# Attention and a feed-forward network in one kernel: the loop over attention units, with a unit's scores and another unit's sums in one run of TensorE

## The chip, the cores and the metric

The kernel runs on one core of one Trainium2 chip. The metric is the device time of one execution in microseconds (us); less is better. Engines are named as the profile names them: PE is TensorE's matmuls and PEld its weight loads, DVE is VectorE, ACT is ScalarE, POOL is GpSimd, and SP is the engine that issues the DMAs.

## The reference

For each of 8 batches and 8 heads there are 576 queries, keys and values of 64 numbers. Scores are masked by blocks of 64 (a query sees the keys of its own block and of earlier ones), go through a softmax, and weigh the values. The heads' results side by side are the rows `x` of a feed-forward network with SiLU.

```python
scores = scale * np.matmul(q, k.transpose(0, 1, 3, 2))          # q, k, v: 8 x 8 x 576 x 64
scores = np.where(block_i >= block_j, scores, -1e9)             # blocks of 64
attn = np.exp(scores - scores.max(-1)); attn /= attn.sum(-1) + 1e-09
x = np.matmul(attn, v).transpose(0, 2, 1, 3).reshape(4608, 512)
h = x @ w_in                                                    # 512 x 2048
out = (h / (1 + np.exp(-h))) @ w_out                            # 2048 x 512
```

## The kernel before

Every fp32 operand of a matmul is split into a high part in TensorE's own 32-bit format and a low part, the rest; a product is then two or three matmuls (high by high, high by low, low by high). ACT makes a high part by a cast (`split_hi`, `v_hi`, `p_hi`, `x_hi`, `g_hi`), and POOL makes the low part by a subtraction (`split_lo`, `v_lo`, `p_lo`, `x_lo`, `g_lo`).

**Attention.** One of 64 units is one head of one batch, for its last 448 queries (the first 128 are done elsewhere, early). A unit's keys stand in five chunks of 128, and only the queries that see a chunk are computed, so its scores are five segments (`SEG`) with 448, 320, 192, 448 and 64 columns, which lie in three PSUM banks (`BANKS`). Its steps are, in the order in which they depend on one another:

- `load`, `split_hi`, `split_lo`: queries and keys, one buffer each for the raw and the split ones;
- `scores`: 10 matmuls on PE into the three banks (each segment with the high and the low part of the queries);
- `max`, `max2`, `sub` on DVE: the maximum over 32 queries at a time, and the difference, into the one tile `T`;
- `exp` on ACT into the tile `p`, one bank at a time; `sums`, and for each second unit `sums2`, on DVE add up `p`;
- `p_hi`, `p_lo`: the two parts `ph` and `pl` of `p`; `load_v`, `v_hi`, `v_lo`: the two parts of the values, in one tile `vc`;
- `pv`: 9 matmuls on PE (`PV`: segment, part of `p`, and how many columns of weights) that sum the values into one PSUM bank `U`;
- `lower` on ACT and `fold` on DVE join the two halves of `U`; `mult` on DVE, for two units at once, divides by the sums (it uses the bank `U` for the spread reciprocals); `x_hi` and `x_lo` write the pair's rows of `x`.

**The feed-forward network** goes over 18 blocks of 256 tokens in 8 steps each. A step is four groups on PE of about equal length: two of `ffn1` (12 matmuls with 256 columns each, from `x` into a PSUM tile `h`, of which there are two), and two of `ffn2` (6 matmuls with 512 columns each, into `o`), these two steps behind the first (`LAG`). Between them are `silu` and `g_hi` on ACT and `g_lo` on POOL (one tile `g`, two tiles `g2`), and at a block's end `output` and `store`. `ffn(n)` issues the next `n` groups with what lies between them.

**Order.** Every engine's queue is in the order of the program, which is fixed (`manual_schedule`). The string `ORDER` is written out by hand and holds the whole beginning: the weights, the first 128 queries, units 0 to 16 in part, and 156 groups of the network. From unit 17 (`TABLE`) on a loop issues one unit per iteration `i`: the scores of unit `i`, the sums of unit `i-1`, the end of unit `i-2`, and 6 or 7 groups of the network (`pace`, from the number of groups issued so far). Groups that are left come behind the loop. A block of the network can start when the last unit that holds its tokens is through `x_lo`.

**Tiles.** `p`, `ph` and `pl` are asked for anew in each unit, under a tag with one buffer: the first write of a new tile waits until every reader of the old one is done. Within one tile waits go by what overlaps.

The lines of the profile: L306 the scores, L385 the sums, L618 `ffn1`, L648 `ffn2`, L250 `max` and `sums`, L259 and L321 and L254 `max2` (L254 also `mult`), L336 to L338 `sub`, L347 `exp`, L353 `p_hi`, L361 and L363 `p_lo`, L278 `split_hi`, L282 and L284 `split_lo`, L290 and L293 `v_hi` and `v_lo`, L390 `lower`, L396 `fold`, L401 `mult`, L418 and L422 `x_hi` and `x_lo`, L625, L631 and L636 `silu`, `g_hi` and `g_lo`, L656 and L661 `output` and `store`.

Of the kernel before, what the change touches and what calls it, by code (L numbers as in the profile page):

```python
# [9 lines left out]
F32 = mybir.dt.float32  # L10
F32R = mybir.dt.float32r
# [3 lines left out]
ALU = mybir.AluOpType  # L15
# [3 lines left out]
B, H, S, D = 8, 8, 576, 64  # L19
DM, DFF = 512, 2048  # L20
P = 128
NQ = S - 2 * D
# [4 lines left out]
NFF = DFF // P  # L27
NSTEP = NFF // 2
TB = 256
CT = DM // P  # L30
NX = 16
EVEN = 4
AHEAD = 152
TABLE = 17
# [3 lines left out]
SEG = [(0, 0, 0, 448), (2, 448, 128, 320), (3, 768, 256, 192), (1, 960, 0, 448), (4, 1408, 384, 64)]  # L38
COLS = 1472

QK = [0, 1, 3, 2, 4]
PV = [(0, 0, 128), (1, 0, 128), (2, 0, 128), (2, 1, 64), (1, 1, 64), (0, 1, 64), (4, 0, 128), (3, 1, 64), (3, 0, 128)]
BANKS = [(0, 448), (448, 960), (960, 1472)]


# [85 lines left out]
def attn_ffn(ctx: ExitStack, tc: tile.TileContext, qk, v, qk0, v0, qk1, v1, w_in, w_out, out):  # L131
    nc = tc.nc
    pool = lambda name, bufs=1, **kw: ctx.enter_context(tc.tile_pool(name=name, bufs=bufs, **kw))
    cp = pool("const")
    sp = pool("work")
    pS = pool("pS", space=PSUM)

    def bank(i):
        return pS.tile([P, 512], F32, tag=f"S{i}", name=f"S{i}")

    pU = pool("pU", space=PSUM)
    pH = pool("pH", bufs=2, space=PSUM)
# [15 lines left out]

    xbuf = cp.tile([P, NX, 2, TB], F32R, name="x")
    x_free = list(range(NX))  # L160
# [3 lines left out]
    ready = set()  # L164
# [91 lines left out]
    def quad_fold(X, src, op):  # L256

        for a in range(4):
            nc.vector.tensor_reduce(out=X[:, :, a], in_=src[32 * a : 32 * a + 32], axis=AX.X, op=op)  # L259

    class Unit:


# [28 lines left out]
        def v_lo(u):  # L292
            nc.gpsimd.tensor_tensor(out=u.vc[:, :, 64:], in0=u.v3, in1=u.vc[:, :, :64], op=ALU.subtract)  # L293

        def scores(u):
            banks = [bank(0), bank(1), bank(2)]

            def ps(c, w, r=P):
                i = max(i for i in range(3) if BANKS[i][0] <= c)
                return banks[i][:r, c - BANKS[i][0] : c - BANKS[i][0] + w]  # L300

            u.ps = ps
            for j, c, q0, w in (SEG[i] for i in QK):
                m = min(P, S - j * P)
                for i, qq in enumerate((u.qh, u.ql)):
                    nc.tensor.matmul(u.ps(c, w, m), u.kk[:, j * P : j * P + m], qq[:, q0 : q0 + w], start=i == 0, stop=i == 1)  # L306

        def max(u):
            ttr(Mx[:, :, 0], blocks32(u.ps(0, NQ)), ALU.max)
# [25 lines left out]
        def sub(u):  # L335
# [4 lines left out]
                    u.half_sub(0)  # L340
            u.half_sub(1)

        def exp(u, k):
            if k == 0:
                u.p = sp.tile([P, COLS], F32, tag="p", name="p")
            c, e = BANKS[k]
            nc.scalar.activation(u.p[:, c:e], T[:, c:e], AF.Exp, scale=SCALE)  # L347

        def p_hi(u, k):
            if k == 0:  # L350
                u.ph = sp.tile([P, COLS], F32R, tag="ph", name="ph")
            c, e = BANKS[k]
            nc.scalar.copy(u.ph[:, c:e], u.p[:, c:e])  # L353

        def p_lo(u, k):

            if k == 0:
                u.pl = sp.tile([P, COLS], F32R, tag="pl", name="pl")
            c, e = BANKS[k]
            e = min(e, SEG[-1][1])  # L360
            nc.gpsimd.tensor_tensor(out=u.pl[:, c:e], in0=u.p[:, c:e], in1=u.ph[:, c:e], op=ALU.subtract)  # L361
            if k == 2:
                nc.gpsimd.tensor_tensor(out=u.ph[64:, e:], in0=u.p[:64, e:], in1=u.ph[:64, e:], op=ALU.subtract)  # L363
# [13 lines left out]
            u.rr = sp.tile([P, NQB], F32, tag="rr", name="rr")  # L377
            nc.vector.reciprocal(out=u.rr, in_=rs)

        def pv(u):  # L380

            U = u.U = pU.tile([P, 512], F32, tag="U", name="U")[:, :NQ]
            for n, (i, pp, m) in enumerate(PV):
                j, c, q0, w = SEG[i]
                nc.tensor.matmul(U[:m, q0 : q0 + w], u.vc[:, j, :m], (u.ph, u.pl)[pp][:, c : c + w], start=n == 0, stop=n == 8)  # L385

        def lower(u):
            a = u.a
# [51 lines left out]
    class Early:  # L440
# [40 lines left out]
        def tiles(u, blk, n):  # L481

            for c in range(CT):
                if (blk, c) not in x_tiles:
# [3 lines left out]
            t = x_tiles[blk, 0]  # L488
            assert [x_tiles[blk, c] for c in range(CT)] == list(range(t, t + CT))
            return xbuf[:, t : t + CT]  # L490

    class First(Early):
# [145 lines left out]
    def ffn2(blk, d, t):  # L638
        g2 = gs[blk, d]
        if d == 0 and t == 0:  # L640
            outs[blk] = [bank(2), pU.tile([P, DM], F32, tag="U", name="o1")] if blk == 0 else [pO.tile([P, DM], F32, tag="o", name="o") for _ in range(2)]
        o = outs[blk][t]
        tk = slice(t * P, t * P + P)
        n = 0
        for f in range(2):
            assert ("out", d, f) in ready
            for gt, wt in ((0, 0), (0, 1), (1, 0)):
                nc.tensor.matmul(  # L648
                    o, g2[:, gt, f, tk], wo[wt][:, 2 * d + f, :],
                    start=d == 0 and n == 0, stop=d == NSTEP - 1 and n == 5,  # L650
                )
                n += 1

    def output(blk, d, t):
        ot = sp.tile([P, DM], F32, tag="ot", name="ot", bufs=2)
        (nc.vector.tensor_copy if late else nc.scalar.copy)(ot, outs[blk][t])  # L656
        outs[blk][t] = ot

    def store(blk, d, t):
        for i, r, w in rows(blk, t):  # L660
            nc.sync.dma_start(out=out[r : r + w, :], in_=outs[blk][t][i : i + w, :])  # L661
# [16 lines left out]
    steps += [(blk, d) for blk in range(2, B * S // TB) for d in range(NSTEP)]  # L678


    work_list = []
# [12 lines left out]
    late = []  # L694
# [24 lines left out]
    units = [Unit(b, h) for b in range(B) for h in range(H)]  # L719
# [11 lines left out]
    for token in ORDER.split():  # L731
        name, _, method = token.partition(".")
        if name.startswith("warm:"):
            warm(int(name[5:]))
        elif method:
            method, _, k = method.partition(":")
# [3 lines left out]
        else:  # L740
            do(name)
    n = len(units)
    for i in range(TABLE, n + 2):
        u = units[i] if i < n else None
        w = units[i - 1] if i <= n else None
        z = units[i - 2] if i > TABLE else None
        pace = 6 + (count[0] <= AHEAD + 7 * (i - TABLE))
        if u:
            u.scores()
            u.max()  # L750
        if z:
            z.fold()
            if z.h % 2:
                z.mult()
        if u:
            u.max2()
        if i + 1 < n:
            units[i + 1].split_hi()
            units[i + 1].split_lo()
            if i + 2 < n:  # L760
                units[i + 2].load()
        ffn(pace - 3)
        if z and z.h % 2:
            z.x_hi()
            z.x_lo()
        if w:
            w.sums()
            w.pv()
        if u:
            u.v_hi()  # L770
            u.v_lo()
            if i + 1 < n:
                units[i + 1].load_v()
            u.sub()
        if w:
            w.lower()
        if u:
            for part in (u.exp, u.p_hi, u.p_lo):
                for k in range(3):
                    part(k)  # L780
        if w and w.h % 2:
            w.sums2()
        late.append(u)
        ffn(3)
        late.pop()
    ffn(10000)


# [38 lines left out]
```

## Time and profile before

| | |
|---|---|
| time, median of 3 runs | 1043.84 us (1043.38 to 1045.03) |
| time of the profiled execution | 1043.46 us |
| span of its profile | 1041.7 us |
| busy: PE, PEld | 1033.4 us (99%), 939.7 us (90%) |
| busy: DVE, ACT, POOL | 763.5 us, 749.1 us, 750.0 us (72 to 73%) |
| granted clock of PE | 1.00 in every slice |

The time is that of the whole execution, and the span goes from the first to the last instruction of its profile. A timeline's row has the start in us from the start of the span, the time from the start of its first to the end of its last instruction, the engine, the line, the operation with the tiles that it writes and reads, and how many instructions in a row it stands for; in brackets stands how long the engine was idle before, and what ended that. A matmul's row lasts longer than the distance to the next one's start, since matmuls are pipelined: it is the starts that show PE's pace.

### The profile page before, as it was taken

What the parts mean: (1) busy time and instruction counts of PE and PEld (TensorE: products, weight loads), DVE (VectorE), ACT (ScalarE), POOL (GpSimd) and SP (SyncE); (2) the same over time, 40 slices, a digit from 0 to 9 for tenths busy, and PEclk for the clock granted to TensorE, in tenths of its full rate; (3) what the DMA queues carried; (4) which work ended last, traced back from release to release, by engine and by line L of the source; (5) the groups of instructions that cost most, each with busy time, mean ns of one, the idle gap of its engine ahead of it and who ended that gap; (6) DMA issues with size and microseconds to landing.
All of it is one profiled execution on the core that took longest, in us unless ns stands there. A gap on an engine that the chain in (4) does not pass through costs nothing.

```text
span 1041.7 us, 20247 instructions
## 1 busy us (share of the span) xinstructions
PE 1033.4 (99%) x7176; PEld 939.7 (90%) x7176; DVE 763.5 (73%) x2232; ACT 749.1 (72%) x1194; POOL 750.0 (72%) x726
## 2 busy tenths in 40 slices
PE   8999999999999999999999999999999999999998
PEld 8988899999899999999999999998999999989987
DVE  7998489999978988888878888888888888700000
ACT  5876578898797888787878787878787777722222
POOL 5766579898897878787878787878787878622221
PEclk9999999999999999999999999999999999999999
DMA  8876223222322222222322222222222222000000
GB/s 291 260 247 189 63 75 90 52 67 74 92 50 84 54 54 74 55 77 59 85 56 74 59 75 55 64 64 54 74 54 75 54 74 54 27 1 21 1 21 21
DMA packets 35044, 79.95 MB, mean 77 GB/s; under 512 B 4736, under 2 KB 12928, under 8 KB 34944
## 3 DMA queue, kind: packets, MB, share of 16 engines
q1 hardware_dynamic: 34944, 78.66, 26.9%
q8 instruction: 57, 0.93, 0.4%
q14 instruction: 43, 0.35, 0.1%
HBM read 69.21 MB, written 9.44 MB: 75 GB/s over the span
## 4 chain that ended last, share of the span: by engine, by line
PE 87%; DVE 4%; POOL 3%; ACT 2%; DMA 2%; issue 1%; SPq 0%; DVEq 0%; POOLq 0%; ACTq 0%
PE h L618 35%; PE o L648 35%; PE S L306 8%; PE U L385 8%; DVE S L227 1%; DVE wm L233 1%; DVE S L223 1%; DMA wst<-in_moe_w_in_dram 1%; POOL pl L361 1%; POOL g L636 1%; DMA T<-in_moe_w_in_dram 0%; PE S L648 0%; ACT L625 0%; DMA qkraw<-in_qk_dram 0%; POOL qh L282 0%
## 5 line engine op out<-in xcount | busy, mean ns | idle before, releaser
L618 PE MATMUL h<-x,wi 128*128 128x256 f32 x3456 | 441.6, 282 | 0.9 <-ACT g L625 0.6
L618 PEld LDWEIGHTS h<-x,wi 128*128 128x128 f32 x3456 | 430.2, 189 | 12.7 <-ACT g L625 1.0
L648 PE MATMUL o<-wo,g 128*128 128x512 f32 x1680 | 424.3, 397 | 0.0
L648 PEld LDWEIGHTS o<-wo,g 128*128 128x128 f32 x1680 | 305.9, 188 | 62.6 <-issue 0.2
L361 POOL TENSOR_TENSOR pl<-p,ph 128x448 fp32r<-128x448 f32 (+1 forms) x192 | 226.0, 1202 | 93.9 <-ACT ph L353 93.5
L636 POOL TENSOR_TENSOR g<-g,g 128x512 fp32r<-128x512 f32 x144 | 186.4, 1295 | 119.8 <-ACT g L631 115.2
L250 DVE TRANSPOSE_TENSOR_REDUCE Mx<-S 64x4 f32<-64x128 f32 (+4 forms) x384 | 135.7, 405 | 94.0 <-PE S L306 93.9
L625 ACT ACTIVATE g<-h 128x512 f32<-128x512 f32 x144 | 86.1, 598 | 126.0 <-POOL g L636 74.6
L631 ACT CAST g<-g 128x512 fp32r<-128x512 f32 x144 | 89.3, 620 | 60.1 <-PE o L648 58.2
L250 DVE TRANSPOSE_TENSOR_REDUCE Dx<-p 128x14 f32<-128x448 f32 (+3 forms) x320 | 122.6, 446 | 0.1
L347 ACT ACTIVATE p<-T 128x512 f32<-128x512 f32 (+1 forms) x192 | 105.6, 604 | 9.5 <-POOL ph L363 8.5
L353 ACT CAST ph<-p 128x512 fp32r<-128x512 f32 (+1 forms) x192 | 104.4, 596 | 1.3 <-PE U L385 1.1
L282 POOL TENSOR_TENSOR qh<-qkraw,qh 64x576 fp32r<-64x576 f32 x64 | 91.6, 1431 | 15.8 <-ACT qh L278 7.1
L306 PE MATMUL S<-qh 128*128 128x448 f32 (+3 forms) x320 | 90.5, 296 | 0.0
L625 ACT ACT_TABLE_LOAD x66 | 84.7, 1283 | 1.4 <-PE h L618 0.3
L306 PE MATMUL S<-ql,qh 128*128 128x448 f32 (+3 forms) x320 | 84.1, 307 | 0.0
L347 ACT ACT_TABLE_LOAD x62 | 79.5, 1283 | 1.6 <-DVE Dx L250 0.5
L284 POOL TENSOR_TENSOR ql<-qkraw,qh 128x448 fp32r<-128x448 f32 x64 | 74.1, 1157 | 5.1 <-PE S L594 0.2
L385 PE MATMUL U<-ph,vc 128*128 128x448 f32 (+3 forms) x320 | 74.1, 297 | 0.0
L278 ACT CAST qh<-qkraw 128x1024 fp32r<-128x1024 f32 x64 | 66.9, 1045 | 8.8 <-PE S L306 4.1
L338 DVE TENSOR_TENSOR T<-S,MR 128x256 f32<-128x256 f32 (+2 forms) x192 | 73.0, 406 | 0.0
L293 POOL TENSOR_TENSOR vc<-vraw,vc 128x320 fp32r<-128x320 f32 x64 | 56.2, 878 | 13.3 <-ACT vc L290 12.8
(120 smaller groups left out, 1120.4 us busy)
## 6 DMA issues: line engine op xcount, KB each, us to landing
qkraw<-in_qk_dram SPq DMA_DIRECT2D x128, 256.0 KB, 3.9
vraw<-in_v_dram SPq DMA_DIRECT2D x64, 160.0 KB, 2.3
wst<-in_moe_w_out_dram SPq DMA_DIRECT2D x15, 512.0 KB, 4.6
out_dram<-ot SPq DMA_DIRECT2D x24, 256.0 KB, 2.9
wst<-in_moe_w_in_dram SPq DMA_DIRECT2D x10, 512.0 KB, 5.3
v<-in_v_dram SPq DMA_DIRECT2D x12, 256.0 KB, 5.2
qk<-in_qk_dram SPq DMA_DIRECT2D x8, 384.0 KB, 5.3
T<-in_moe_w_in_dram SPq DMA_DIRECT2D x6, 512.0 KB, 4.5
```

The source lines that it names most:

```text
L250: nc.vector.tensor_reduce(out=out, in_=in_, axis=AX.X, op=op, apply_transpose=True)
L282: nc.gpsimd.tensor_tensor(out=u.qh[64:, NQ:], in0=u.raw[64:, NQ:], in1=u.qh[64:, NQ:], op=ALU.subtract)
L306: nc.tensor.matmul(u.ps(c, w, m), u.kk[:, j * P : j * P + m], qq[:, q0 : q0 + w], start=i == 0, stop=i == 1)
L347: nc.scalar.activation(u.p[:, c:e], T[:, c:e], AF.Exp, scale=SCALE)
L353: nc.scalar.copy(u.ph[:, c:e], u.p[:, c:e])
L361: nc.gpsimd.tensor_tensor(out=u.pl[:, c:e], in0=u.p[:, c:e], in1=u.ph[:, c:e], op=ALU.subtract)
L385: nc.tensor.matmul(U[:m, q0 : q0 + w], u.vc[:, j, :m], (u.ph, u.pl)[pp][:, c : c + w], start=n == 0, stop=n == 8)
L618: nc.tensor.matmul(h[:, f, :], wi[wt][:, c, w], x[:, xt, :], start=n == 0, stop=n == 3 * CT - 1)
L625: nc.scalar.activation(g, hs.pop((blk, d)), AF.Silu)
L631: nc.scalar.copy(g2[:, 0], g)
L636: nc.gpsimd.tensor_tensor(out=g2[:, 1], in0=g, in1=g2[:, 0], op=ALU.subtract)
L648: nc.tensor.matmul(o, g2[:, gt, f, tk], wo[wt][:, 2 * d + f, :], start=d == 0 and n == 0, stop=d == NSTEP - 1 and n == 5,)
```

## The change

- `scores` of unit `i` takes the unit two before it along: seven of that unit's nine sums come ahead of the ten scores, and two behind them, in another order (`JOINT`). The loop's sums are thus those of unit `i-2`, not of unit `i-1`, and the run of sums by itself is gone (it stays for the last two units).
- `p`, `ph` and `pl` become three tiles that the loop keeps (`place`), so a write of one bank's columns waits only for the readers of those columns. `p_hi` and `p_lo` go by banks 1, 0, 2.
- In an iteration the queues now hold: `max`, `max2`; then `v_hi`, `v_lo`, `load_v`, `p_hi`, `p_lo` of unit `i-1` (they were those of unit `i`, behind `exp`); `lower`, `fold` of unit `i-2`; one group; `split_hi`, `sub`, `split_lo`, `load`; `mult`; one group; `x_hi`, `x_lo`; all groups but four; `sums`; `exp`; two groups; `sums2`.
- The copies of `output` go to DVE only in the part with all groups but four.
- The very last `ffn2` group is done in two parts of 256 columns: the left one goes on in its bank, the right one's last sums go to a bank of their own. ACT copies the first bank out, DVE adds the right part, and each half has its own store.

```diff
+JOINT = [(0, 0, 128), (2, 0, 128), (2, 1, 64), (1, 1, 64), (1, 0, 128), (4, 0, 128), (3, 1, 64), (0, 1, 64), (3, 0, 128)]
...
-        def scores(u):
+        def scores(u, other=None):
...
+            if other is not None:
+                other.pv(JOINT[:7])
+            for i in QK:
+                j, c, q0, w = SEG[i]
                 m = min(P, S - j * P)
...
+            if other is not None:
+                other.pv(JOINT[7:], 7)
...
+        def place(u, tag, kind):
+
+            if tag not in places:
+                t = sp.tile([P, COLS], kind, tag=tag, name=tag)
+                if not keep:
+                    return t
+                places[tag] = t
+            return places[tag]
...
-            if k == 0:
-                u.p = sp.tile([P, COLS], F32, tag="p", name="p")
+            if not hasattr(u, "p"):
+                u.p = u.place("p", F32)
...
-        def pv(u):
-
-            U = u.U = pU.tile([P, 512], F32, tag="U", name="U")[:, :NQ]
-            for n, (i, pp, m) in enumerate(PV):
+        def pv(u, products=PV, first=0):
+
+            if first == 0:
+                u.U = pU.tile([P, 512], F32, tag="U", name="U")[:, :NQ]
+            for n, (i, part, m) in enumerate(products, first):
                 j, c, q0, w = SEG[i]
-                nc.tensor.matmul(U[:m, q0 : q0 + w], u.vc[:, j, :m], (u.ph, u.pl)[pp][:, c : c + w], start=n == 0, stop=n == 8)
+                nc.tensor.matmul(u.U[:m, q0 : q0 + w], u.vc[:, j, :m], (u.ph, u.pl)[part][:, c : c + w], start=n == 0, stop=n == 8)
...
         tk = slice(t * P, t * P + P)
...
+        split = t and (blk, d) == (NBLK - 1, NSTEP - 1)
+        if split:
+            outs[blk][t] += [(bank(0)[:, :HD], slice(HD, DM))]
+        for i, (o, c) in enumerate(outs[blk][t]):
+            if split and i == 0:
+                o, c = o[:, :HD], slice(0, HD)
...
+        (o, c), *right = outs[blk][t]
+        (nc.vector.tensor_copy if late else nc.scalar.copy)(ot, o)
+        outs[blk][t] = [(ot, c)]
+        for o, c in right:
+            nc.vector.tensor_tensor(out=ot[:, c], in0=o, in1=ot[:, c], op=ALU.add)
+            outs[blk][t] = [(ot, slice(0, HD)), (ot, c)]
...
+    keep.append(True)
     for i in range(TABLE, n + 2):
         u = units[i] if i < n else None
-        w = units[i - 1] if i <= n else None
+        w = units[i - 1] if TABLE < i <= n else None
         z = units[i - 2] if i > TABLE else None
         pace = 6 + (count[0] <= AHEAD + 7 * (i - TABLE))
         if u:
-            u.scores()
+            u.scores(z)
             u.max()
+            u.max2()
+        else:
+            z.pv()
+        if w:
+            w.v_hi()
+            w.v_lo()
+            if u:
+                u.load_v()
+            for part in (w.p_hi, w.p_lo):
+                for k in (1, 0, 2):
+                    part(k)
         if z:
+            z.lower()
             z.fold()
-            if z.h % 2:
-                z.mult()
-        if u:
-            u.max2()
+        ffn(1)
         if i + 1 < n:
             units[i + 1].split_hi()
+        if u:
+            u.sub()
+        if i + 1 < n:
             units[i + 1].split_lo()
             if i + 2 < n:
                 units[i + 2].load()
-        ffn(pace - 3)
+        if z and z.h % 2:
+            z.mult()
+        ffn(1)
+        late.append(u)
         if z and z.h % 2:
             z.x_hi()
             z.x_lo()
-        if w:
-            w.sums()
-            w.pv()
+        ffn(pace - 4)
+        if i <= n:
+            units[i - 1].sums()
         if u:
-            u.v_hi()
-            u.v_lo()
-            if i + 1 < n:
-                units[i + 1].load_v()
-            u.sub()
-        if w:
-            w.lower()
-        if u:
-            for part in (u.exp, u.p_hi, u.p_lo):
-                for k in range(3):
-                    part(k)
-        if w and w.h % 2:
-            w.sums2()
-        late.append(u)
-        ffn(3)
+            for k in range(3):
+                u.exp(k)
         late.pop()
+        ffn(2)
+        if i <= n and units[i - 1].h % 2:
+            units[i - 1].sums2()
     ffn(10000)
```

## Rows read from the trace of the kernel before

**Rows 1.** The page, part 1: busy us, share of the span, instructions.

```profile
PE 1033.4 (99%) x7176; PEld 939.7 (90%) x7176; DVE 763.5 (73%) x2232; ACT 749.1 (72%) x1194; POOL 750.0 (72%) x726
```

**Rows 2.** PE's waits: in total, times, longest.

```profile
PE h L618 <- POOL x L422: 0.3, 1, 0.3
```

**Rows 3.** Windows, busy us: units 41, 42 (7 groups each) and 18 (6).

```profile
610.75:623.44 12.69, 12.69 (x86) 11.73 (x85) 10.02 (x29) 11.27 (x19) 11.12 (x11) 1.00 0.24 58
623.44:636.13 12.69, 12.69 (x86) 11.75 (x85) 10.79 (x36) 8.99 (x15) 8.55 (x8) 1.00 0.33 95
323.18:334.44 11.26, 11.26 (x70) 10.03 (x69) 10.16 (x34) 10.21 (x17) 9.79 (x9) 1.00 0.14 39
```

**Rows 4.** PE's timeline: a run of sums, and the group after it.

```profile
605.18 0.60 PE L385 MATMUL U<-ph,vc 128*128 128x448 f32 x3
...
606.53 1.57 PE L618 MATMUL h<-x,wi 128*128 128x256 f32 x12
```

**Rows 5.** PE's and PEld's timelines: two usual network matmuls, scores, what follows.

```profile
597.83 0.39 PE L618 MATMUL h<-x,wi 128*128 128x256 f32 x2
...
610.75 0.36 PE L306 MATMUL S<-qh 128*128 128x448 f32 x1
...
612.08 0.22 PE L306 MATMUL S<-ql,qh 128*64 128x64 f32 x1
612.14 0.48 PE L618 MATMUL h<-x,wi 128*128 128x256 f32 x2
...
612.11 0.42 PEld L618 LDWEIGHTS h<-x,wi 128*128 128x128 f32 x3
```

**Rows 6.** Timeline of POOL and ACT around unit 41.

```profile
611.20 3.52 POOL L361 TENSOR_TENSOR pl<-p,ph 128x448 fp32r<-128x448 f32 x3 [2.56 <-ACT ph L353]
...
615.20 1.30 POOL L636 TENSOR_TENSOR g<-g,g 128x512 fp32r<-128x512 f32 x1
616.58 1.43 POOL L282 TENSOR_TENSOR qh<-qkraw,qh 64x576 fp32r<-64x576 f32 x1
...
619.26 1.30 POOL L636 TENSOR_TENSOR g<-g,g 128x512 fp32r<-128x512 f32 x1
...
621.78 0.88 POOL L293 TENSOR_TENSOR vc<-vraw,vc 128x320 fp32r<-128x320 f32 x1
...
619.64 0.46 ACT L290 CAST vc<-vraw 128x320 fp32r<-128x320 f32 x1
...
623.50 1.59 ACT L353 CAST ph<-p 128x448 fp32r<-128x448 f32 x3
```

**Rows 7.** Timeline of DVE in unit 41.

```profile
613.78 0.63 DVE L396 TENSOR_TENSOR xu<-U,t 64x448 f32<-64x448 f32 x1
614.45 0.66 DVE L254 STREAM_TRANSPOSE U<-rr 128x448 f32<-128x448 f32 x1
...
615.68 0.90 DVE L259 TENSOR_REDUCE Xm<-Mx 32x14 f32<-32x70 f32 x4
...
618.07 1.91 DVE L250 TRANSPOSE_TENSOR_REDUCE Dx<-p 128x14 f32<-128x448 f32 x5
619.90 0.58 DVE L336 TENSOR_TENSOR T<-S,MR 128x448 f32<-128x448 f32 x1
...
621.60 0.27 DVE L331 TENSOR_TENSOR T<-S,MR 64x128 f32<-64x128 f32 x1
```

**Rows 8.** Timelines of PE and POOL: block 12's first group, iteration 49.

```profile
720.73 1.33 PE L618 MATMUL h<-x,wi 128*128 128x256 f32 x10
721.98 1.43 POOL L422 TENSOR_TENSOR x<-xu,x 128x64 fp32r<-128x64 f32 x3
...
722.34 0.38 PE L618 MATMUL h<-x,wi 128*128 128x256 f32 x1 [0.28 <-POOL x L422]
```

**Rows 9.** The end's timeline, and a DVE operation from PSUM by form (busy, mean ns).

```profile
1038.29 0.58 ACT L656 COPY ot<-o 128x512 f32<-128x512 f32 x1 [0.82 <-PE o L648]
...
L338 DVE TENSOR_TENSOR T<-S,MR 128x256 f32<-128x256 f32 x64 | 26.1, 409 | 0.0
```

More of the change, by code (lines that the diff above doesn't have):

```diff
@@ L29 @@
 TB = 256
+NBLK = B * S // TB
+HD = DM // 2
 CT = DM // P
@@ L259, in quad_fold @@
             nc.vector.tensor_reduce(out=X[:, :, a], in_=src[32 * a : 32 * a + 32], axis=AX.X, op=op)
+    places, keep = {}, []
     class Unit:
@@ L302, in scores @@
             u.ps = ps
-            for j, c, q0, w in (SEG[i] for i in QK):
+            if other is not None:
+                other.pv(JOINT[:7])
+            for i in QK:
+                j, c, q0, w = SEG[i]
                 m = min(P, S - j * P)
-                for i, qq in enumerate((u.qh, u.ql)):
-                    nc.tensor.matmul(u.ps(c, w, m), u.kk[:, j * P : j * P + m], qq[:, q0 : q0 + w], start=i == 0, stop=i == 1)
+                for part, q in enumerate((u.qh, u.ql)):
+                    nc.tensor.matmul(u.ps(c, w, m), u.kk[:, j * P : j * P + m], q[:, q0 : q0 + w], start=part == 0, stop=part == 1)
+            if other is not None:
+                other.pv(JOINT[7:], 7)
         def max(u):
@@ L349, in p_hi @@
         def p_hi(u, k):
-            if k == 0:
-                u.ph = sp.tile([P, COLS], F32R, tag="ph", name="ph")
+            if not hasattr(u, "ph"):
+                u.ph = u.place("ph", F32R)
             c, e = BANKS[k]
@@ L355, in p_lo @@
         def p_lo(u, k):
-            if k == 0:
-                u.pl = sp.tile([P, COLS], F32R, tag="pl", name="pl")
+            if not hasattr(u, "pl"):
+                u.pl = u.place("pl", F32R)
             c, e = BANKS[k]
@@ L640, in ffn2 @@
         if d == 0 and t == 0:
-            outs[blk] = [bank(2), pU.tile([P, DM], F32, tag="U", name="o1")] if blk == 0 else [pO.tile([P, DM], F32, tag="o", name="o") for _ in range(2)]
-        o = outs[blk][t]
-        tk = slice(t * P, t * P + P)
[L644 to L652, printed above, removed]
+            new = lambda: pO.tile([P, DM], F32, tag="o", name="o")
@@ new lines, in ffn2 @@
+            whole = slice(0, DM)
+            if blk == 0:
+                outs[blk] = [[(bank(2), whole)], [(pU.tile([P, DM], F32, tag="U", name="o1"), whole)]]
+            else:
+                outs[blk] = [[(new(), whole)] for _ in range(2)]
+        tk = slice(t * P, t * P + P)
+        split = t and (blk, d) == (NBLK - 1, NSTEP - 1)
[4 more added lines that the diff above has]
+                o, c = o[:, :HD], slice(0, HD)
+            n = 0
+            for f in range(2):
+                assert ("out", d, f) in ready
+                for gt, wt in ((0, 0), (0, 1), (1, 0)):
+                    nc.tensor.matmul(
+                        o, g2[:, gt, f, tk], wo[wt][:, 2 * d + f, c],
+                        start=(d == 0 or i > 0) and n == 0, stop=d == NSTEP - 1 and n == 5,
+                    )
+                    n += 1
@@ L654, in output @@
     def output(blk, d, t):
         ot = sp.tile([P, DM], F32, tag="ot", name="ot", bufs=2)
-        (nc.vector.tensor_copy if late else nc.scalar.copy)(ot, outs[blk][t])
-        outs[blk][t] = ot
+        (o, c), *right = outs[blk][t]
[4 more added lines that the diff above has]
+            outs[blk][t] = [(ot, slice(0, HD)), (ot, c)]
@@ L659, in store @@
     def store(blk, d, t):
-        for i, r, w in rows(blk, t):
-            nc.sync.dma_start(out=out[r : r + w, :], in_=outs[blk][t][i : i + w, :])
+        for ot, c in outs[blk][t]:
+            for i, r, w in rows(blk, t):
+                nc.sync.dma_start(out=out[r : r + w, c], in_=ot[i : i + w, c])
     def rows(blk, t):
@@ L677, in attn_ffn @@
     steps += [(0, d) for d in range(EVEN + 1, NSTEP)] + [(1, d) for d in range(EVEN, NSTEP)]
-    steps += [(blk, d) for blk in range(2, B * S // TB) for d in range(NSTEP)]
+    steps += [(blk, d) for blk in range(2, NBLK) for d in range(NSTEP)]
     work_list = []
@@ L748, in attn_ffn @@
         if u:
-            u.scores()
+            u.scores(z)
             u.max()
+            u.max2()
+        else:
+            z.pv()
[7 more added lines that the diff above has]
+                    part(k)
         if z:
+            z.lower()
             z.fold()
-            if z.h % 2:
-                z.mult()
-        if u:
-            u.max2()
+        ffn(1)
         if i + 1 < n:
             units[i + 1].split_hi()
+        if u:
+            u.sub()
+        if i + 1 < n:
             units[i + 1].split_lo()
```

## The prediction

> **What bounds the kernel now.** I read the page's busy shares first: PE is busy 99% of the span, the other three engines 72 to 73% [rows 1]. That alone proves little, since a matmul's row is longer than its share of the pipeline, so I read PE's waits next. In the whole loop of units there is one wait that another engine ends, 0.3 us for POOL's low part of `x` [rows 2]. Then windows from one run of scores to the next: an iteration with seven groups of the network lasts 12.69 us, whatever the other engines do in it (POOL 11.12 us in one, 8.55 us in the next), and one with six groups lasts 11.26 us [rows 3]. So the loop lasts as long as PE's own queue, and DVE, ACT and POOL have 1.5 to 4 us to spare per iteration. From this follow two ways for the change to move the time: PE's instructions get shorter by standing in another order, or PE begins to wait for an engine whose work now comes later. The last reading is the starts of the matmuls, where a run of sums begins and ends [rows 4], and a run of scores [rows 5].
>
> **PE's own time: the joint run.** The sums go from 605.18 to 606.53, 1.35 us [rows 4]. The scores begin at 610.75 and the network's next matmul at 612.14, 1.39 us. But two network matmuls behind the scores take 0.48 us from the start of the first to the end of the second, and two usual ones 0.39 us [rows 5], so the scores cost 0.09 us more than their own run; together 2.82 us. What costs this: the last two matmuls of the scores have only 64 columns. The last starts at 612.08, and the weight load for the network's matmul starts at 612.11, only after it; in the load's row three loads, each about 0.19 us long, cover 0.42 us, so they start 0.11 to 0.12 us apart [rows 5]. A load of 128 columns thus takes 0.11 us, and a matmul of 64 columns (0.028 us, from 0.203 us for 448) is too short to hide it. The last matmul costs 0.11 instead of 0.028 us, 0.083 us lost.
>
> In the joint run the matmul behind it is a sum with the low part of `p`, whose weights are 64 columns: half a load, 0.055 us (it is also the distance 612.08 to 612.14 that two such loads leave [rows 5]), so 0.027 us are lost. The other short matmul, segment 4's sum, is followed by a 64-column load in both orders. The saving is 0.083 - 0.027 = 0.056 us per joint run. Units 18 to 63 have one: 46 x 0.056 = **-2.6 us**. Bounds: 0 (if the lost time only moves to the new seams, 512 or 256 columns against sums) and -4.1 us (46 x 0.09, nothing lost any more). The row is nearest to -2.6.
>
> The Trainium skill has a rule that speaks against this term: TensorE: Matmul & The Clock Gate, Part 2, says that PE's queue pulls a weight load ahead of running matmuls when it goes to the background weight buffer. By it the load for the network would already be under way during the longer matmuls, the old order would lose nothing, and this term would be 0. The trace does not bear it out here: the load starts at 612.11, behind the start of the last score [rows 5], so at most one load is ahead.
>
> **PE's new waits.** Take the start of a joint run as 0. It lasts 2.82 - 0.056 = 2.76 us; its scores start at about 0.94 (seven sums, 1984 columns at 0.203 us per 448, and 0.03). A group lasts (12.69 - 2.82) / 7 = 1.41 us, an iteration 12.63 us.
>
> *ACT, POOL.* `v_hi` overwrites the one `vc`, so it waits for the last sum: 2.76 and some 0.19 us until it is through, 2.95. It is in front of `p_hi` in ACT's queue, so keeping `ph` by banks gives `p_hi` nothing. `v_hi` 0.46 and `v_lo` 0.88: 4.3. `p_lo` takes 4.0 (611.20 to 615.20): 8.3; `split_lo` 2.68 (616.58 to 619.26): **11.0** [rows 6], and 12.4 where a `g_lo` (616.58 - 615.20 = 1.38) is ahead of it. ACT's `p_hi` (1.59 [rows 6]) keeps ahead of `p_lo`. `split_lo` moves from 8.5 us behind the start of the scores (619.26 - 610.75) to 10.1 or 11.4 us.
>
> *DVE.* `max` ends 3.03 us after the scores' start (613.78): 3.97. `max2` 2.39 (615.68 to 618.07), `fold` 0.6, `sub` 1.97 (619.90 to 621.87), `mult` 1.23 (614.45 to 615.68): 6.4, 7.0, 8.9, 10.2; `sums` 1.83 (618.07 to 619.90) [rows 7]: 12.0, or 10.8 in an iteration without `mult`. `fold` needs `lower` from ACT at about 5.6 and has it. The banks are free at 8.9 and wanted at 13.6; `U` is free at 10.2 and wanted at 12.6. No wait.
>
> Three places in which PE could wait:
>
> 1. *Queries and keys.* The next scores start at 12.63 + 0.94 = 13.6, the first with the low part 0.2 later. `split_lo` ends at 11.0 to 12.4, and later by what `g_lo` of the iteration before pushed `v_lo` back (its `exp` ends some 0.6 behind `sums`, and SiLU and its cast come behind `exp`; up to 0.9). So 0.5 to 2.8 us remain: no wait with seven groups. Iterations 17 to 20 have six groups (156 + 6n against 152 + 7n), 11.26 us, while POOL's work goes to 9.8 to 11.1 us [rows 3]; what it lacks there adds up to 0 to 1.3 us of wait. I take **+0.6 us**.
> 2. *Block 12's first group.* 156 groups are issued when the loop begins; iteration 49 begins with group 376, and step 96, block 12, begins with group 4 x 96 - 4 = 380, the fifth of this iteration. It needs unit 47, whose `x_lo` is in the same iteration. Before, PE lost there: ten matmuls from 720.73 at 0.118 us each, the eleventh due at 721.91 and begun at 722.34, so 0.43 us [rows 8]. After, the fifth group begins at 2.76 + 4 x 1.41 = 8.4, and its eleventh matmul, at 9.6, reads that low part. `x_hi` is ready at 10.4 (behind `mult`), but `x_lo` stands behind `split_lo` in POOL's queue: 11.0 and 0.36 for its first piece (722.34 - 721.98 [rows 8]) are 11.4; with 0 to 0.9 carried over, a wait of 1.8 to 2.7 us. I take 2.1, **+1.7 us** against before.
> 3. *The network's own tiles.* SiLU goes behind `x_hi` or `exp` now; an `h` is wanted again six groups (8.5 us) later. Late by 2 to 5 us, it is covered.
>
> **Edits at nothing.** Kept `p`, `ph`, `pl`: `exp` of a bank waits for the sums of that bank, about 1.2 us earlier than for all (`sums` 1.83 less its first 0.6); ACT's spare time covers either. `load` waits for `split_lo` in SP's queue as before and `load_v` for `v_lo`; both follow by some 2 us and are wanted later by as much (estimates from the positions above). `output` on DVE in the middle part: two copies per block, in DVE's spare 1.9 us (12.69 - 10.79 [rows 3]). If that cover is gone, `sums`, then `exp`, then `v_hi` and `p_lo` are late, and it ends in wait 1.
>
> **The end.** Now ACT's copy of 0.58 us follows the last matmul [rows 9], then the store. After, DVE's add of 256 columns follows (0.41 us, the nearest row [rows 9]): -0.17 us, and the second store has half the bytes. The parts' 12 matmuls of 256 columns take 12 x 0.118 = 1.42 us instead of a group's 1.41. I take **-0.3 us**, bounds +0.2 (the second store queues behind the first) and -0.6.
>
> **The sum.** -2.6 + 0.6 + 1.7 - 0.3 = -0.6 us. The profiled execution took 1043.46 us, of which 1041.7 is the span; that gives 1042.9 us. It lies 0.4 us below the median of the runs, so against the median 1043.84 - 0.6 = **1043.2 us**. What a measurement of this kernel can tell from no change is about 0.2%, 2.1 us: faster is below 1041.8, slower above 1045.9.
>
> **The rivals.**
>
> *The waits do not grow* (faster). If POOL reaches `x_lo` of unit 47 by 9.6 + 0.6, and the six-group iterations keep up, what is left is -2.6 - 0.3 and at most 0.2 of wait: 1041.0 us. For it: only two places in 46 iterations are short, POOL has time in half of the iterations [rows 3], and DVE and ACT are then no limit. Against it: four operations of POOL in a row of known length stand ahead of `x_lo` [rows 6]. It decides if `v_lo` starts 1.5 us earlier than I have it.
>
> *The split of queries and keys becomes the bound* (slower). In an iteration with `mult` POOL has 11.1 us of work [rows 3] in 12.63, SiLU, `x_hi` and `exp` come late on ACT, and `g_lo` is then pushed in front of `v_lo`. If this chain is more than 0.5 us later than worked out, PE waits for `split_lo` in every second iteration; at 0.2 us each in 22 of them, +4.4 us: 1043.2 + 4.4 = 1047.6 us. For it: `split_lo` has by far the least to spare of everything that PE needs. Against it: each wait of PE gives POOL its time back.
>
> *The joint run saves nothing* (the rule above, or losses at the new seams): 1043.2 + 2.6 = 1045.8 us, no change that can be told. Against it stands the 0.09 us of [rows 5].
>
> **How the numbers follow.** Forecast 0.52, waits do not grow 0.27, split becomes the bound 0.17, saving absent 0.04. Faster: the second, 0.27. Slower: the third, 0.17. No change: the others, 0.56. The range goes from 1040.6 (all of the saving, less than the old wait at block 12) to 1046.6 us (the third rival at half its price and more); about 0.09 is left out on each side. The forecast's own range is 1041.8 to 1045.
>
> **What would show it.** In the profile after: a run of sums and scores of 2.76 us with no long first network matmul behind it; iterations of 12.63 us; a wait of PE for L422's successor of about 2 us in iteration 49, and a few tenths for `split_lo` in iterations 19 to 21. Wrong would be: waits of PE on `split_lo` in many iterations, iterations still of 12.69 us without a wait, or no wait at block 12.

## The result, and the profile after

The kernel after takes 1046.53 us (median of 13 runs, 1044.53 to 1047.51), the kernel before 1043.84 (13 runs): a ratio of 1.0023, 95% interval 1.0015 to 1.0030. It is slower by 2.7 us, and just over the 0.2% that the prediction took as the bound of a change. The 13 runs fall into two groups: four at 1044.5 to 1045.1 us, nine at 1046.4 to 1047.5. The profiled one is of the first group: 1044.95 us, span 1043.2, which is 1.49 us more than the profiled execution of before.

The page's busy shares (us, share of the span, instructions) still look like [rows 1]:

```profile
PE 1032.9 (99%) x7182; PEld 937.1 (90%) x7182; DVE 773.9 (74%) x2233; ACT 749.3 (72%) x1194; POOL 748.5 (72%) x726
```

PE's waits in the loop of units answer to [rows 2] (L639 is the network's first product, L315 the scores; us in total, times, longest; the last line is the same view for the weight loads):

```profile
PE h L639 <- ACT x L439: 1.1, 1, 1.1
PE S L315 <- POOL ql L290: 1.0, 2, 0.6
PE h L639 <- POOL x L443: 0.6, 1, 0.6
...
PEld S L315 <- POOL ql L290: 4.4, 11, 1.0
```

Before, there was one wait of 0.3 us. Now the queries' low part `ql`, the second operation of `split_lo`, is late eleven times. Windows from scores to scores answer to [rows 3]: iterations 41, 43 and 44, then 20, 47 and 49 (start and end, length, then busy us of PE, PEld, DVE, ACT, POOL, granted clock, DMA):

```profile
610.54:623.15 12.61, 12.61 (x86) 11.66 (x85) 11.36 (x31) 8.23 (x15) 10.95 (x12) 1.00 0.28 72
635.76:648.52 12.76, 12.76 (x80) 11.34 (x79) 10.38 (x30) 9.41 (x18) 11.18 (x13) 1.00 0.31 82
648.52:661.16 12.64, 12.64 (x80) 11.43 (x79) 11.01 (x36) 12.49 (x19) 9.64 (x10) 1.00 0.11 30
345.15:357.23 12.08, 11.47 (x69) 9.92 (x68) 10.34 (x34) 11.63 (x18) 11.63 (x13) 1.00 0.24 58
686.38:699.69 13.31, 12.89 (x80) 11.33 (x79) 10.88 (x33) 9.99 (x18) 11.72 (x13) 1.00 0.27 72
712.33:727.20 14.87, 13.17 (x87) 11.81 (x85) 10.17 (x29) 10.47 (x19) 11.43 (x13) 1.00 0.32 83
```

Where nothing is waited for, an iteration lasts 12.61 to 12.64 us instead of 12.68 to 12.70: 0.067 us less on the mean, 3.1 us over 46 iterations. Nearly every fourth iteration (43 is one, there are nine) is 0.15 to 0.25 us longer than that, about 1.7 us together; iteration 20 is longer by 0.88 (12.08 against 11.26 - 0.06), iteration 47 by 0.69, and iteration 49 by 2.24 (0.54 before).

PE's timeline of a joint run answers to [rows 4, 5]:

```profile
609.60 0.46 PE L406 MATMUL U<-ph,vc 128*128 128x448 f32 x2
...
611.92 0.40 PE L406 MATMUL U<-pl,vc 128*64 128x448 f32 x1
612.16 0.36 PE L406 MATMUL U<-ph,vc 128*128 128x448 f32 x1
612.37 1.80 PE L639 MATMUL h<-x,wi 128*128 128x256 f32 x14
```

From 609.60 to 612.37 it is 2.77 us, and the network's matmuls behind it have their usual pace (14 in 1.80 us: 13 steps of 0.117 and one row of 0.28).

Block 12's first group, to be held against [rows 8]:

```profile
720.13 1.42 POOL L288 TENSOR_TENSOR qh<-qkraw,qh 64x576 fp32r<-64x576 f32 x1
721.63 1.14 POOL L290 TENSOR_TENSOR ql<-qkraw,qh 128x448 fp32r<-128x448 f32 x1
721.80 0.75 ACT L439 CAST x<-xu 128x64 fp32r<-128x64 f32 x3 [3.83 <-DVE xu L422]
722.09 0.39 PE L639 MATMUL h<-x,wi 128*128 128x256 f32 x1 [1.08 <-ACT x L439]
722.72 1.44 POOL L443 TENSOR_TENSOR x<-xu,x 128x64 fp32r<-128x64 f32 x3
723.10 1.93 PE L639 MATMUL h<-x,wi 128*128 128x256 f32 x14 [0.61 <-POOL x L443]
```

`x_hi` (L439) waits for the closing product on DVE, then `x_lo` (L443) stands behind both operations of `split_lo` on POOL. PE stops twice with one matmul between.

The end, against [rows 9]: PE's last row before, then two rows of after.

```profile
1029.68 8.58 PE L648 MATMUL o<-wo,g 128*128 128x512 f32 x36
...
1039.22 0.88 PE L679 MATMUL S<-wo,g 128*128 128x256 f32 x6
...
1040.19 0.42 DVE L691 TENSOR_TENSOR ot<-S,ot 128x256 f32<-128x256 f32 x1 [121.36 <-PE S L679]
```

The span ends at 1043.2, 3.1 us behind the last matmul (1039.22 + 0.88); before, it ended 3.5 us behind PE (1029.68 + 8.58 = 1038.26, to 1041.7).

The sum for the first group: -3.1 (PE's own time) + 0.88 + 0.69 + 1.7 (queries) + 1.70 (block 12, 2.24 - 0.54) - 0.35 (end) = +1.5 us, where 1.49 is measured. The other group's 1.9 us are not in this trace.

### The profile page after: what moved, and what is told of

The parts are those of the page before. It is cut to its first block, busy times and chain, and to the rows that moved or that the text cites. A ratio compares the mean times of both kernels' runs of the same rounds, so it can differ in the third digit from the quotient of the medians.

```text
span 1043.2 us, 20172 instructions
## 1 busy us (share of the span) xinstructions
PE 1032.9 (99%) x7182; PEld 937.1 (90%) x7182; DVE 773.9 (74%) x2233; ACT 749.3 (72%) x1194; POOL 748.5 (72%) x726
## 4 chain that ended last, share of the span: by engine, by line
PE 79%; POOL 8%; DVE 4%; DMA 3%; ACT 3%; issue 2%; SPq 0%; DVEq 0%; POOLq 0%; ACTq 0%
PE h L639 32%; PE o L679 32%; PE S L315 8%; PE U L406 7%; POOL pl L381 3%; DMA wst<-in_moe_w_in_dram 2%; POOL g L657 1%; POOL qh L288 1%; DVE S L231 1%; DVE S L227 1%; DVE wm L237 1%; POOL ql L290 1%; POOL vc L299 1%; ACT L646 1%; PE S L679 1%
## 5 line engine op out<-in xcount | busy, mean ns | idle before, releaser
L639 PEld LDWEIGHTS h<-x,wi 128*128 128x128 f32 x3456 | 429.4, 188 | 15.0 <-ACT x L439 1.3
L639 PE MATMUL h<-x,wi 128*128 128x256 f32 x3456 | 437.3, 281 | 2.3 <-ACT x L439 1.1
L679 PE MATMUL o<-wo,g 128*128 128x512 f32 (+1 forms) x1680 | 419.3, 396 | 0.0
L367 ACT ACTIVATE p<-T 128x512 f32<-128x512 f32 (+1 forms) x192 | 105.4, 604 | 9.2 <-POOL ph L383 8.4
L315 PE MATMUL S<-qh 128*128 128x448 f32 (+3 forms) x320 | 90.4, 295 | 0.0
L315 PE MATMUL S<-ql,qh 128*128 128x448 f32 (+3 forms) x320 | 85.3, 311 | 1.0 <-POOL ql L290 1.0
```

The costliest lines, as they stand in the source:

```text
L639: nc.tensor.matmul(h[:, f, :], wi[wt][:, c, w], x[:, xt, :], start=n == 0, stop=n == 3 * CT - 1)
L679: nc.tensor.matmul(o, g2[:, gt, f, tk], wo[wt][:, 2 * d + f, c], start=(d == 0 or i > 0) and n == 0, stop=d == NSTEP - 1 and n == 5,)
```

## The experiments

Each line is a median, with its number of runs and the ratio to the kernel before on the same chip (1044.09 us for the first four, 1044.08 for the others).

| kernel | us | ratio, 95% interval |
|---|---|---|
| end alone, on before | 1043.90 (11) | 0.9998 (0.9989 to 1.0007) |
| two runs | 1086.12 (5) | 1.0400 (1.0385 to 1.0414) |
| `ql` on DVE | 1053.49 (4) | 1.0088 (1.0074 to 1.0102) |
| block 12 first | 1043.12 (11) | 0.9990 (0.9981 to 0.9999) |
| order of the scores | 1043.72 (11) | 0.9995 (0.9986 to 1.0004) |
| order and block 12 | 1040.92 (6) | 0.9973 (0.9961 to 0.9984) |
| tiles not kept | 1052.54 (5) | 1.0080 (1.0067 to 1.0093) |
| after, again | 1046.65 (11) | 1.0023 (1.0014 to 1.0032) |

**After, again: what the second group is.** No edit.

> The kernel after itself, to have times on the same chip as the other runs and another profile. Theory: in the runs near 1046.5 to 1047 us PE's granted clock falls to its lower level for 3 to 4 us behind the 2.2 us wait before block 12 (as it does in the traces of the two kernels with longer waits there, 0.79, 0.50 and 0.86 in three stretches of 2 us), which costs 1.6 to 2 us; in runs near 1045 us it stays at 1.00 there. Rival: the clock stays at 1.00 in the loop in both groups, and the 1.9 us lie elsewhere (the start, the transfers, the end).

Its profiled run took 1046.39 us and lies in the upper group. Windows of its iteration 49 (the column behind POOL's is the granted clock):

```profile
720.00:722.00 2.00, 0.93 (x9) 0.72 (x8) 1.97 (x5) 0.30 (x2) 1.87 (x2) 1.00 0.00 0
722.00:724.00 2.00, 1.35 (x6) 1.16 (x7) 1.52 (x5) 1.95 (x5) 2.00 (x4) 0.83 0.02 6
724.00:726.00 2.00, 2.00 (x12) 2.00 (x11) 0.00 (x0) 1.99 (x4) 1.31 (x2) 0.50 0.92 256
726.00:728.00 2.00, 2.00 (x9) 1.65 (x9) 0.00 (x0) 1.97 (x4) 0.00 (x0) 0.82 0.00 0
```

The waits are those of the first trace (1.1, 0.6 and 1.0 us, the same rows), but behind them the clock falls to its lower level (0.50, which is 1.2 of 2.4 GHz) for a part of the first and the third and all of the second of three windows: 0.17, 0.50 and 0.18 of 2 us are missing, 1.7 us of work at full speed. The iteration lasts 16.41 us here instead of 14.87, 1.54 more; the whole run is 1.44 us longer. So the theory holds for this pair of traces: the same wait, then the clock falls or does not. It does not explain all of the upper group. Ten of all 24 runs of this kernel have a mean granted clock of 0.998; their median is 1046.8 us, and none is below 1046.39. The other fourteen, at 0.999 or 1.00, have a median of 1045.8 us, 1.7 to 2.0 above before's medians, which is near the +1.5 of the sum. But they reach from 1044.53 to 1047.51: beside some upper ones (1046.53, 1046.65) stands 1.00, and the eleven new runs (1044.9 to 1048.6) lie less clearly in two groups. What those lost stays open; the runs of before spread by 2 us as well. The Trainium skill (TensorE: Matmul & The Clock Gate, Part 1) says that the gate looks at PE's recent activity in a rhythm that does not start with the kernel, so that the same kernel can meet it differently. That the clock fell in one of two runs behind the same wait agrees with that, though no run here shows the rhythm itself.

**Block 12 first.** In iteration 49 alone, the last unit's closing product and `x` go ahead:

```diff
             z.lower()
             z.fold()
+        early = i == 49
+        if early:
+            z.mult()
+            z.x_hi()
+            z.x_lo()
         ffn(1)
...
-        if z and z.h % 2:
+        if z and z.h % 2 and not early:
```

> The kernel after, but in iteration 49 alone unit 47's closing product, x's copy and x's rest stand ahead of the next unit's query and key work and of the subtraction of the maxima, on VectorE, ACT and POOL; nothing is left out. Theory: PE's wait before block 12 (1.25 us for x's copy on ACT and 0.99 us for x's rest on POOL) goes, since unit 50's keys have 4 us of room there: 1044.95 - 2.1 = 1042.9 us. If that wait is also what puts 9 of after's 13 runs 1.5 to 2.5 us above the other four (PE at the lower granted clock for some us behind it), then nearly all runs lie within 0.7 us of 1042.9 and the median is 1042.9. Rival: the second group has another cause, the runs still fall into two groups 1.9 us apart, and the median is 1044.5. Second rival: the wait only moves to the queries and keys of unit 50, and the time stays at 1045 to 1046.5.

The window of iteration 49:

```profile
711.91:724.53 12.62, 12.62 (x87) 11.66 (x86) 10.16 (x29) 9.10 (x17) 10.73 (x13) 1.00 0.23 56
```

The wait is gone, 14.87 to 12.62 us, and it has not moved: the queries' waits stay at 4.4 us in eleven places. The median falls by 3.4 to 3.5 us against after (1046.53 and 1046.65), which is more than the wait's 2.24. The 1.2 us above it fit the clock in part, since of 11 runs none has a mean granted clock below 0.999, where ten of after's 24 are at 0.998; what else is in them is not shown. Nine of the 11 runs lie within 0.7 us of the 1042.9 forecast, and two groups are no longer seen. The runs still spread from 1042.2 to 1044.4, as those of before do (1043.06 to 1045.48).

**Order of the scores.** Three products with the upper part of the queries go ahead of the first one that needs `ql`:

```diff
+QUERIES = [(0, 0), (1, 0), (3, 0), (0, 1), (1, 1), (3, 1), (2, 0), (2, 1), (4, 0), (4, 1)]
...
-            u.ps = ps
+            u.ps, u.late = ps, other is not None
...
-            for i in QK:
+            for i, part in QUERIES if u.late else [(i, part) for i in QK for part in range(2)]:
...
-                for part, q in enumerate((u.qh, u.ql)):
...
+                q = (u.qh, u.ql)[part]
```

The new order holds in joint runs alone.

> The kernel after, but in a joint run the scores' products stand in another order: the three first segments with the upper part of the queries (448, 320 and 448 columns), then the same three with the rest of the queries, then the two last segments as before. The first product that needs the tile that POOL makes last starts 0.35 us later (0.148 + 0.203 us of products moved ahead of it). Theory: that much of each wait for the queries goes: 0.88 to 0.53 us in iteration 20, 0.69 to 0.34 in 47, the ten of 0.1 to 0.24 to nothing, together 3.27 to 0.87 us; 1044.95 - 2.4 = 1042.5 us in the quicker group of runs, and 1044.1 in the other, since the block 12 wait stays. Rival: the first bank of scores is ready 0.35 us later, VectorE's maxima with it, and what follows on VectorE, ACT and POOL, so the wait comes back in the next iteration and the time stays at 1044.5 to 1046.5.

The weight loads' waits, order of the scores alone:

```profile
PEld S L316 <- POOL ql L291: 1.0, 2, 0.6
```

Of eleven waits two are left (iterations 20 and 47), 4.4 us are now 1.0, and the time is 2.8 to 2.9 us lower than after's. The maxima on DVE, 0.35 us later, did not bring the wait back. Block 12's wait is still there (1.1 and 0.7 us), and the granted clock behind it is 0.59 and 0.56 in two windows of 2 us of this profiled run. Against after's profiled run with the same fall of the clock (1046.39) this one (1043.86) is 2.5 us shorter, where 2.4 were forecast.

**Order and block 12 together.** Both edits.

> The kernel after with both: the scores' products in the order of the run before, and in iteration 49 unit 47's closing product and x's tiles ahead of the next unit's query and key work. Theory: both of PE's waits go, the gains add: the median of the kernel with the block 12 edit alone, 1043.1, less 2.4 = 1040.7 us (1040.2 to 1041.3), 3 us under the kernel before, with no second group of runs. Rival: as for the run before, the wait comes back in the next iteration: 1043 us.

1040.92 us, 5.7 us under after and 3.2 us under before, interval 0.9961 to 0.9984. Alone the two edits gave 3.5 and 2.9 us, together 5.7: the gains add up but for some 0.7 us, which is within the spread of the runs. Two of the six runs (1042.53, 1042.86) lie above the forecast's range, so the second group that it ruled out is not shown to be gone. PE's waits in the loop, all that is left:

```profile
PE S L316 <- POOL ql L291: 0.3, 1, 0.3
```

So the change is worth about 0.3% once its two kinds of wait are mostly taken away.

**Two runs: what the joint run itself saves.**

```diff
-            u.scores(z)
+            u.scores()
             u.max()
             u.max2()
-        else:
+        ffn(1)
+        if z:
             z.pv()
...
-        ffn(1)
```

> The kernel after with the joint run undone: a unit's scores by themselves, then one network group, then the other unit's sums in the old order of products; the rest of the loop's order stays. Theory: the joint run is worth 0.07 us in every iteration, by which the undisturbed iterations of after (12.62 us from scores to scores) are shorter than those of before (12.69); they go back to 12.68 to 12.70, which over 46 iterations is 3.1 us, so about 1044.95 + 3.1 = 1048 us where the waits of after stay as they are. Rival: the shorter iterations come from somewhere else than the run's place beside the other (from the network's products, say), they stay at 12.62, and the time stays within 1 us of after's.

PE's timeline where this kernel does not wait:

```profile
782.69 1.57 PE L639 MATMUL h<-x,wi 128*128 128x256 f32 x12
784.10 0.37 PE L315 MATMUL S<-qh 128*128 128x448 f32 x1
...
785.49 1.67 PE L639 MATMUL h<-x,wi 128*128 128x256 f32 x12
786.99 0.61 PE L406 MATMUL U<-ph,vc 128*128 128x448 f32 x3
...
788.34 0.39 PE L679 MATMUL o<-wo,g 128*128 128x512 f32 x1
```

Scores 1.39 us (784.10 to 785.49), sums 1.35 (786.99 to 788.34), and the twelve network matmuls behind the scores take 1.67 us where twelve ahead of them take 1.57: 2.84 us, against 2.77 for the joint run. So the saving in the products is there, 0.07 us with this reading's rounding. What I expected of the time was wrong by 38 us, because I counted only the products. In the weight loads' waits of this kernel

```profile
PEld S L315 <- POOL ql L290: 25.4, 25, 1.0
PEld S L315 <- POOL qh L288: 13.3, 21, 1.3
```

one sees where it went: 38.7 us, against 4.4 in after. With the sums one group later, `v_hi` and all that ACT and POOL do behind it start later by that group, and `split_lo` comes too late in most iterations. The joint run is worth little on PE, but the order around it rests on it.

**`ql` on DVE.**

```diff
-            nc.gpsimd.tensor_tensor(out=u.ql, in0=u.raw[:, :NQ], in1=u.qh[:, :NQ], op=ALU.subtract)
+            engine = nc.vector if u in on_dve else nc.gpsimd
+            engine.tensor_tensor(out=u.ql, in0=u.raw[:, :NQ], in1=u.qh[:, :NQ], op=ALU.subtract)
...
+    on_dve = {u for i, u in enumerate(units) if i > TABLE and (i % 2 or i == 20)}
```

> The kernel after, but the subtraction that makes the rest of the queries (128x448, the last thing POOL does ahead of the next scores) runs on VectorE for every second unit (those whose iteration has no closing product) and for unit 20; nothing is left out. Theory: PE's waits for this tile (3.27 us in all: 0.88 in iteration 20, 0.69 in 47, 0.1 to 0.24 in each fourth iteration) go, because POOL's queue in front of the scores is 1.15 us shorter where it was late by at most 0.9: 1044.95 - 3.0 = 1042 us (1041.6 to 1042.6) in the quicker of after's two groups of runs, the block 12 wait stays 2.2 us. Rival: VectorE has no room for 0.6 us more, the subtraction of the maxima and the exponentials come later, and the wait moves to the rest of p: 1044.5 us or more.

The time is on the rival's side, 1053.49 us, though not through the rest of `p` as the rival had it. Timeline rows of POOL and DVE:

```profile
711.10 2.65 POOL L382 TENSOR_TENSOR pl<-p,ph 128x448 fp32r<-128x448 f32 x2
712.66 1.58 DVE L291 TENSOR_TENSOR ql<-qkraw,qh 128x448 fp32r<-128x448 f32 x1
713.84 0.59 POOL L384 TENSOR_TENSOR ph<-p,ph 64x64 fp32r<-64x64 f32 x1
...
433.07 0.61 DVE L291 TENSOR_TENSOR ql<-qkraw,qh 128x448 fp32r<-128x448 f32 x1
433.00 0.86 POOL L384 TENSOR_TENSOR ph<-p,ph 64x64 fp32r<-64x64 f32 x1
```

The same operation takes 0.61 us at 433.07 and 1.58 us at 712.66, where it starts inside one of POOL's; and POOL's small one takes 0.59 and 0.86 us instead of 0.32 (in after, mean of 64: 0.317). Of the 24 subtractions that moved to DVE, eleven take 0.60 to 0.61 us and thirteen 0.98 to 1.91. The two engines wait for each other. The Trainium skill (SBUF — State Buffer, Who interferes with whom) has the rule: a VectorE operation with two inputs in SBUF contends with a GpSimd operation that reads SBUF, because its second input comes through read ports that the two engines share. The trace agrees; I had not weighed it. In before and after, DVE's subtractions have one input in PSUM, and nothing of this is seen: POOL's small one takes 0.32 us at most. The lateness then ends on DVE's closing product and on POOL:

```profile
PE U L407 <- DVE xu L423: 2.0, 1, 2.0
PE h L640 <- POOL x L444: 1.9, 1, 1.9
PE h L640 <- ACT x L440: 1.4, 1, 1.4
```

Behind the last two the clock falls as well (0.79, 0.50 and 0.86 in the three windows of 2 us that follow, the ones that the expectation of after's second run speaks of). Since that cost has its own cause, this run says little on the queries' wait; the order of the scores settles that.

**Tiles not kept.**

```diff
-    keep.append(True)
```

> The kernel after without the kept tiles: each unit takes p and its two parts as new tiles again, freed as a whole. The prediction costed the kept tiles at nothing. Theory: the users of the last unit's p end in the order in which the next unit's banks are written, so nothing on PE's path moves by more than 0.3 us, and the times are those of after (1045 and 1046.8 us in two groups). Rival: exponentials that wait for the last of POOL's products on p instead of for their bank come 1 us later, the next p's rest is late for the sums, and the time rises to 1048 us or more.

The time is the rival's: 1052.54 us, 5.9 above after. Its wait is another one, for the sums on DVE and not for POOL's products. ACT's waits in the loop, with new tiles:

```profile
ACT L367 <- DVE Dx L254: 14.5, 13, 1.7
```

and in after:

```profile
ACT L367 <- DVE Dx L254: 0.4, 1, 0.4
```

L367 is the exponential (here its table load, which is issued with it), Dx the sums. Without kept tiles it waits for all of a unit's sums. Of these 14.5 us a part arrives at `split_lo` (the weight loads' waits for `ql` are 7.9 us instead of 4.4) and at block 12 (PE waits 2.8 us there instead of 1.7).

**The end alone, on the kernel before.**

> The kernel before with the end in two parts alone (the last products into two 128x256 targets, the copy of the left half under the products of the right, one addition and two stores per half); nothing in the loop is changed. Theory: the end part of the trace is 0.35 us shorter after the change (3.14 us from PE's last matmul to the span's end against 3.49), and this belongs to the split alone, so 1043.84 - 0.35 = 1043.5 us. Rival: the end is shorter because of what the new loop leaves on the queues, and the split by itself gives nothing: 1043.8 us.

```diff
+        split = t and (blk, d) == (NBLK - 1, NSTEP - 1)
+        if split:
+            outs[blk][t] += [(bank(0)[:, :HD], slice(HD, DM))]
```

(with the copy, the addition and the two stores of the change). The times do not tell the two apart: -0.2 us with an interval of -1.1 to +0.7. In its trace PE ends at 1040.21 (a run of six from 1039.33, 0.88 us) and the span at 1043.3: 3.1 us, as in after, and not 3.5 as in before. So by the traces the end is worth 0.35 us and belongs to the split.

## Why the prediction was wrong

- **What bounds the kernel, and from where a loss must come**: right. PE's queue is the length of the loop, and all that was lost came through its waits.
- **The joint run, -2.6 us**: right, somewhat small. 2.77 us was forecast as 2.76; the iterations gave 0.067 us each, 3.1 in all. The Trainium skill's rule on weight loads pulled ahead, by which this term would be 0, is not borne out here: the time was saved.
- **Place 1, queries and keys: "no wait with seven groups"**: this is the step that failed, with the sign of being wrong that the prediction named. There is a wait in nearly every fourth iteration, and 0.69 us in iteration 47, 2.4 us together. The six-group iterations, taken at 0.6, cost 0.88. The rows that show it are ACT's and POOL's timelines around iteration 42 (its joint run starts at 622.22):

```profile
620.00 0.67 ACT L439 CAST x<-xu 128x256 fp32r<-128x256 f32 x2 [3.83 <-DVE xu L422]
...
621.83 1.28 ACT L367 ACT_TABLE_LOAD   x1
623.12 1.62 ACT L367 ACTIVATE p<-T 128x448 f32<-128x448 f32 x3
624.76 1.28 ACT L646 ACT_TABLE_LOAD   x1
626.05 0.60 ACT L646 ACTIVATE g<-h 128x512 f32<-128x512 f32 x1
626.55 0.45 ACT L296 CAST vc<-vraw 128x320 fp32r<-128x320 f32 x1
...
627.08 0.88 POOL L299 TENSOR_TENSOR vc<-vraw,vc 128x320 fp32r<-128x320 f32 x1 [3.58 <-ACT vc L296]
627.90 3.54 POOL L381 TENSOR_TENSOR pl<-p,ph 128x512 fp32r<-128x512 f32 x3
...
631.92 1.29 POOL L657 TENSOR_TENSOR g<-g,g 128x512 fp32r<-128x512 f32 x1
633.29 1.43 POOL L288 TENSOR_TENSOR qh<-qkraw,qh 64x576 fp32r<-64x576 f32 x1
634.80 1.15 POOL L290 TENSOR_TENSOR ql<-qkraw,qh 128x448 fp32r<-128x448 f32 x1
```

  I let `v_hi` start when the last sum is through, 2.95 us into the run, and allowed 0 to 0.9 us for what ACT carries over. It starts at 4.33: the exponentials come after the previous iteration's `x_hi` (620.00), SiLU and its cast, and each change between exponential and SiLU costs a table load of 1.28 us. Two of them, 2.56 us, stand in the chain, and my working has none. By these rows ACT would without them be done with the rest at about 624.0 (an estimate, 626.55 - 2.57), ahead of the 625.17 at which the last sum is through; no run takes the loads away. `v_lo` ends at 5.7 us, not 4.3; the lengths behind it were right (`p_lo`, `g_lo` and `split_lo` take 8.0 us with their gaps), and so `ql` is ready at 13.7 us, when the first product that needs it is due at 13.7 and its load 0.2 us earlier. Seven groups against steps of four groups repeat after four iterations, so this queue with a `g_lo` in it comes in every fourth. The nine iterations ahead of these waits are alike: `v_hi` starts at 4.32 to 4.42 us behind the two loads, and `ql` is ready at 13.73 to 13.83 (4.88 and 14.27 ahead of iteration 47). All waits but two cost PE less than 0.25 us, therefore 0.35 us of other products ahead of `ql` took nearly all of it away.
- **Place 2, block 12**: right, 2.24 us against 2.1, through the operations that it named; that PE would first stop for `x_hi`, ready at 10.4 us as worked out, it did not say, and this does not change the total. What it lacked is the second price of such a wait, the fall of the granted clock, 1.5 us where it was traced, and about 1 us between the medians of the runs with and without a lower mean clock.
- **Place 3, and the edits at nothing**: no wait of PE for SiLU, loads or copies is seen in the loop. For the kept tiles the named cover (ACT's spare time) does not exist: taken away, they cost 5.9 us, by the chain that the prediction gave for that case.
- **The end, -0.3**: right, -0.35.
- **The rivals**: the second one came true in part: the chain is more than 0.5 us later than worked out and PE waits for `split_lo`, at a smaller price than I gave it (2.4 us, not 4.4). Its condition was met (`v_lo` 1.4 us late), though in every fourth iteration and not every second, and not by a `g_lo` in front of `v_lo`: where one stands there (iterations 24 and 28, `v_lo` through at 6.6 and 6.5 us) none is left behind `p_lo`, and `ql` is in time (13.2 and 13.1 us).

From 1043.2 to the 1046.53 measured 3.3 us are missing: +2.4 for place 1, +0.3 for the six groups and -0.5 for the joint run are +2.2 us, which turns the -0.6 of the forecast into the +1.6 that the profiled pair shows to 0.1. The other 1.1 us lie between the profiled run and the median. The fall of the clock in ten of 24 runs is a part of them; for the rest, and for the median run itself (1046.53 us at a mean clock of 1.00), the cause stays open.

## What to carry to other kernels

When work is moved between queues, follow the engine that looks idle through its whole queue, with every operation in it, table loads too: ACT is 28% idle here, and its order still sets when POOL starts, and POOL when PE goes on. Where a tile comes a few tenths too late for PE, put products that don't need it ahead of those that do; here that gave back 2.8 us at the median, and no other wait came up for it. A wait of PE can cost more than its length, so take the longest one away first.

## What the runs showed of the hardware that I had not expected

- PE at full work, then 2.2 us of waiting in two pieces, and the granted clock fell to 0.50 in one run and stayed at 1.00 in another of the same kernel: 1.5 us of difference.
- DVE and POOL held each other up where both read two SBUF operands: 0.61 us became 1.58, and 0.32 became 0.59 to 0.86.
